# Three products of zeros ahead of the first loads, one load issued by ScalarE, and all scaled copies of the mixing on VectorE

## The chip, the cores and the metric

The kernel runs on one core of one Trainium2 chip. The core has four engines that compute, each with a queue of its own that it works off in order: TensorE (PE in the profile, its weight loads PEld), VectorE (DVE), ScalarE (ACT) and GpSimd (POOL). SyncE (SP) issues the transfers between HBM and the core's own memory (SBUF); PE writes its results to PSUM, in eight banks. Engines wait for each other by semaphores. The metric is the time of one execution on the device, in microseconds, the median of several runs.

## The reference

An attention without softmax is followed by a channel mix.

```python
def _attn_ref(q, k, v):
    scores = scale * np.matmul(q, k.transpose(0, 1, 3, 2)) - np.log(S)
    attn = 1.0 / (1.0 + np.exp(-scores))
    return np.matmul(attn, v)
...
def _moe_ref(x, mu_k, mu_r, w_k, w_v, w_r):
    x_prev = np.concatenate([np.zeros((B, 1, D)), x[:, :-1, :]], axis=1)
    xk = mu_k * x + (1.0 - mu_k) * x_prev
    xr = mu_r * x + (1.0 - mu_r) * x_prev
    k = np.maximum(xk @ w_k, 0.0)
    v = k * k @ w_v
    r = 1.0 / (1.0 + np.exp(-(xr @ w_r)))
    return r * v
```

The shapes: 8 batches, 12 heads, 448 positions, 64 elements a head, so 768 channels; `w_k` is 768 x 1024, `w_v` 1024 x 768, `w_r` 768 x 768, and the weights come as 64-bit floats.

## The kernel before

The 96 heads are laid out as 48 pairs of heads (n), two heads of 64 elements on the 128 partitions, with positions along the free axis. The kernel has two phases, each with a plan of its own.

**Attention.** The loop (lines 460 to 475) takes two pairs, n and n + 1, at a time and seven steps j over the 448 keys, 64 at a time. `score` (line 309) issues four matmuls, whose quarters fill the 128 x 128 array together, into one of two PSUM buffers `sc`, and ACT makes the sigmoid of both halves into one of three buffers `pf` (line 320). `weigh` (line 325), two steps behind, multiplies `pf` with the values `vn` and sums over the seven steps in a PSUM bank `av`; there are four such banks, so a bank is written again two rounds later. Operands here are fp32, and each call of matmul leaves two records on PE and two weight loads.

After the last step of a round `gather` (line 336) mixes each pair with its predecessor in time, once with `mu_r` and once with `mu_k`: POOL clears the first column of a buffer `xo` (a ring of eight), a scaled copy of `av`, shifted by one column, is written to it (line 345 on DVE for `mu_r`, line 347 on ACT for `mu_k`), DVE adds `mu * av` (line 348), and a transfer stores the result to HBM. Beside this, DVE turns the 64-bit weights into fp32 bits (lines 212 to 216) and forms sums of their quarters (line 244). For the first weight, `w_r`, ACT casts the rounded part into a `slot` (line 289) and DVE makes the rest (line 290). Spare time is given to the first operands of the second phase (lines 413 and 414).

**Products.** Three products with `w_r`, `w_k` and `w_v` (stages 0 to 2), each over four slices s of two batches, run as seven half-sized products each (`multiply`, line 518), every one as three passes of rounded and remaining parts. Their sums are taken from PSUM by DVE and ACT (`evacuate`, line 558).

**What sets the order.** Nothing is issued as the loops run. Each operation is given to a `Plan` with its engine, its cost in ns, its priority (lower first), and the buffers that it reads and writes. `order` (line 49) plays the plan through: an engine that is free takes the ready operation of the lowest priority number; a result is ready for another operation `WAIT` = 170 ns after its producer's planned end (none from PE to PE), and a transfer after a modelled 300 GB/s and 1300 ns. The operations are then issued in the order of their planned starts, which sets each engine's queue. Semaphores are put in by the framework from what each operation reads and writes, so the plan decides order alone.

**The start.** The framework's own preamble ends near 0.7 us. Then DVE clears a small tile `warm` (line 141) and ACT makes a sigmoid of it (line 142), which has its table loaded early. All transfers are issued by SP through `dma` (line 200), 500 ns each in the plan. `load` (line 297) brings one pair: the first 64 key columns with all queries (512 columns, 256 KB), the remaining keys (384 columns, 192 KB), and the values (224 KB). For the first two pairs `late` orders them: both first pieces, both second pieces, both values. The first score step needs the first pieces of pairs 0 and 1, the next one the second pieces too.

Of the kernel before, what the change touches and what calls it, by code (L numbers as in the profile page):

```python
# [10 lines left out]
AF = mybir.ActivationFunctionType  # L11
# [11 lines left out]
class Plan:  # L23
# [7 lines left out]
    def op(self, engine, cost, prio, run, reads, writes, dma=None):  # L31
        i = len(self.ops)
        deps = set()
        for r in reads:
            if r in self.writer:
                deps.add(self.writer[r])
        for w in writes:
            if w in self.writer:
                deps.add(self.writer[w])
            deps.update(self.readers.get(w, ()))  # L40
        for r in reads:
            self.readers.setdefault(r, []).append(i)
        for w in writes:
            self.writer[w] = i
            self.readers[w] = []
        deps.discard(i)
        self.ops.append(Op(engine, cost, prio, run, deps, dma))

    def order(self):
        import heapq  # L50
        ops = self.ops
        left = [len(o.deps) for o in ops]
        users = [[] for _ in ops]
        for i, o in enumerate(ops):
            for d in o.deps:
                users[d].append(i)
        at = [0.0] * len(ops)
        free, ready, waiting = {}, {}, []
        for i, o in enumerate(ops):
            free[o.engine] = 0.0  # L60
            ready.setdefault(o.engine, [])
            if not left[i]:
                heapq.heappush(waiting, (0.0, i))
        bus, start = self.bus, {}
        now = 0.0
        while len(start) < len(ops):
            while waiting and waiting[0][0] <= now:
                i = heapq.heappop(waiting)[1]
                heapq.heappush(ready[ops[i].engine], (ops[i].prio, i))
            for e in free:  # L70
                if free[e] <= now and ready[e]:
                    i = heapq.heappop(ready[e])[1]
                    o = ops[i]
                    start[i] = now
                    free[e] = now + o.cost
                    end = now + o.cost
                    if o.dma is not None:
                        bus = max(bus, end + 700) + o.dma
                        end = bus + 1300
                    for u in users[i]:  # L80
                        gap = 0 if ops[u].engine == e == "PE" else self.WAIT
                        at[u] = max(at[u], end + gap)
                        left[u] -= 1
                        if not left[u]:
                            heapq.heappush(waiting, (at[u], u))
            nxt = [free[e] for e in free if ready[e]] + ([waiting[0][0]] if waiting else [])
            if nxt:
                now = max(now, min(nxt)) if min(nxt) > now else now
        self.start = start
        return sorted(start, key=lambda i: (start[i], i))  # L90
# [8 lines left out]
def attention_then_channel_mix(  # L99
# [15 lines left out]
    nc = tc.nc  # L115
    P = 128
# [3 lines left out]
    D = v.shape[-1]  # L120
# [17 lines left out]
    dram = ctx.enter_context(tc.tile_pool(name="dram", bufs=1, space=DRAM))  # L138

    warm = const.tile([P, 2], F32, name="warm")  # L140
    nc.vector.memset(warm, 0.0)
    nc.scalar.activation(warm[:, 1:], warm[:, :1], AF.Sigmoid)
    mur = const.tile([P, NJ], F32, name="mur")
    muk = const.tile([P, NJ], F32, name="muk")
    omr = const.tile([P, NJ], F32, name="omr")
# [2 lines left out]
    xr_d = [dram.tile([P, NJ, S], F32, name=f"xr_d{b}") for b in range(B)]  # L148
# [8 lines left out]
    def ring(pool, name, bufs, shape, dtype):  # L157
        return [pool.tile(shape, dtype, name=f"{name}{i}") for i in range(bufs)]
# [14 lines left out]
    av = ring(psum, "av", 4, [P, 512], F32)  # L173
    sc = ring(psum, "sc", 2, [P, 2, 512], F32)

    raw = ring(apool, "raw", RAW, [P, 2 * S], F32)
    vn = ring(apool, "vn", RAW, [P, NV, D], F32)
    pf = ring(apool, "pf", PFB, [P, 2, S], F32)
    xo = ring(apool, "xo", 8, [P, S], F32)

    plan = Plan()
    op = plan.op
    SP, PE, ACT, DVE, POOL = "SP", "PE", "ACT", "DVE", "POOL"
# [4 lines left out]
    def act(n, sbuf=False, ptr=False):  # L188
        return 51 + 0.834 * n + 42 * sbuf + 93 * ptr

    def dve(n, fast=False, ptr=False):
        return 69 + n / (1.92 if fast else 0.96) + 61 * ptr
# [7 lines left out]
    def dma(dst, src, prio, reads, writes):  # L200
        ns = dst.shape[0] * math.prod(dst.shape[1:]) * 4 / 300
        op(SP, 500, prio, lambda: nc.sync.dma_start(dst, src), reads, writes, dma=ns)
# [94 lines left out]
    def load(n, at):  # L297
        i = n % RAW
        late = 0.5 * (n < 2)
        for a, c in enumerate((slice(0, D + S), slice(D + S, 2 * S))):  # L300
            dma(raw[i][:, c], qk[n][:, c], at + late * a, [], [("raw", i, a)])
        dma(vn[i], v[n], at + 2 * late, [], [("vn", i)])

    half = [slice(h * D, (h + 1) * D) for h in range(2)]
# [17 lines left out]
    def bank(m):  # L322
        return m % 4
# [12 lines left out]
    def gather(n, at):  # L336
        b, j = divmod(n, NP)
        x, X = av[bank(n)], ("av", bank(n))
        for mu, om, dst, key in ((mur, omr, xr_d, "xr_d"), (muk, omk, xk_d, "xk_d")):
            u = nxo[0] % len(xo)  # L340
            nxo[0] += 1
            y, Y = xo[u], ("xo", u)
            op(POOL, 200, at, lambda y=y: nc.gpsimd.memset(y[:, 0:1], 0.0), [], [Y])
            if key == "xr_d":
                op(DVE, dve(S, ptr=True), at, lambda y=y, om=om: nc.vector.tensor_scalar_mul(y[:, 1:], x[:, :S - 1], om[:, j:j + 1]), [X, ("om", key)], [Y])  # L345
            else:
                op(ACT, act(S, ptr=True), at, lambda y=y, om=om: nc.scalar.mul(y[:, 1:], x[:, :S - 1], om[:, j:j + 1]), [X, ("om", key)], [Y])  # L347
            op(DVE, dve(S, ptr=True), at, lambda y=y, mu=mu: nc.vector.scalar_tensor_tensor(y, x[:, :S], mu[:, j:j + 1], y, ALU.mult, ALU.add), [X, Y], [Y])  # L348
            dma(dst[b][:, j], y, at, [Y], [(key, n)])

# [93 lines left out]
    for n in range(4):  # L444
        load(n, -9 + n // 2 * 2)
# [14 lines left out]
    for t in range(T + LAG):  # L460
        n, j = t // NV * 2, t % NV
        if t < T:
            if j == 0:
                for _ in range(1 + (n % 6 == 4)):
                    convert_next(n + 4, n - 2 if n else None)
            score(n, j, t, n + j / NV)
        if t < LAG:
            continue
        n, j = (t - LAG) // NV * 2, (t - LAG) % NV
        weigh(n, j, t - LAG, n + j / NV)  # L470
        if j == NV - 1:
            for m in (n, n + 1):
                gather(m, m)
                if m + 4 < N:
                    load(m + 4, n + 0.5)
# [22 lines left out]
    op = plan.op  # L498
# [89 lines left out]
    at = 0  # L588
# [49 lines left out]
```

## Time and profile before

| What | Value |
|---|---|
| Time, median of 3 runs | 824.85 us (824.68 to 825.09) |
| Time of the profiled execution | 824.86 us |
| Its span, first to last instruction | 823.1 us |
| Instructions | 15181 |
| Read from HBM, written to it | 109.06 MB, 69.73 MB |

The span is what the profile shows; some 1.8 us of the execution's time lie outside it. In the profile a group is a line of the kernel with its engine, operation and tiles; behind "idle before" stands what ended the idle time of the engine ahead of it. A timeline's row gives the start and the length in us, the engine, the line and the tiles, and how many instructions were merged into it. A row of a window table gives the window, its length, and per engine the busy time with the number of records that lie in it, wholly or in part. A matmul's record is longer than the distance to the next one, since matmuls overlap.

### The profile page before, as it was taken

The page shows a single profiled execution, that of the slowest core. Times are in us where ns is not written, and L with a number is a line of the kernel's source. Part 1 is how long each engine was busy: PE and PEld are TensorE (multiplying, and loading weights), DVE is VectorE, ACT ScalarE, POOL GpSimd, SP SyncE. Part 2 cuts the span into 40 slices and gives each one's busy share as a digit, 9 for nine tenths or more (in the row PEclk, how much of TensorE's full clock was granted, in tenths as well). Part 3 has the DMA queues.
Part 4 walks back from the last instruction along what each step waited for, and adds up shares of the span by engine and source line. Part 5 has one row for each costly group of instructions (what it writes and reads, how often), then busy time and mean ns, then how long its engine had stood idle before and what let it go on. Part 6 is the DMA issues. An engine that isn't in the chain of part 4 may idle for free.

```text
span 823.1 us, 15181 instructions
## 1 busy us (share of the span) xinstructions
PE 812.9 (99%) x5460; PEld 622.9 (76%) x5460; DVE 615.1 (75%) x1152; ACT 467.1 (57%) x791; POOL 10.3 (1%) x100
## 2 busy tenths in 40 slices
PE   8999999999999999999999999999999999999997
PEld 3433334343334999999999999999999999999997
DVE  0888687685654898989999639376697795977955
ACT  5788776767676553546584747647694233333320
POOL 0000000000000000000000000000000000000000
PEclk9999999999999999999999999999999999999999
DMA  8787789999872948576879542422865545755414
GB/s 274 267 312 265 268 272 317 335 352 308 287 262 90 304 161 264 169 247 206 328 228 316 195 146 102 151 96 102 288 217 188 164 145 190 225 179 178 143 39 156
DMA packets 94715, 179.80 MB, mean 218 GB/s; under 512 B 10544, under 2 KB 75312, under 8 KB 94640
## 3 DMA queue, kind: packets, MB, share of 16 engines
q1 hardware_dynamic: 94640, 178.83, 64.7%
q8 instruction: 43, 0.70, 0.4%
q14 instruction: 32, 0.26, 0.1%
HBM read 109.06 MB, written 69.73 MB: 217 GB/s over the span
## 4 chain that ended last, share of the span: by engine, by line
PE 90%; DVE 4%; ACT 2%; DMA 2%; issue 1%; SPq 0%; ACTq 0%; DVEq 0%
PE xb L530 39%; PE yb L530 29%; PE sc L317 12%; PE av L329 11%; DVE xo L348 1%; ACT pf L320 1%; DMA raw<-in_qk 1%; ACT xo L347 1%; DMA wraw<-in_moe_w_r 1%; DVE wbit L216 0%; DVE wbit L215 0%; DVE wbit L214 0%; DVE xo L345 0%; DMA wk_o<-wbit 0%; DVE wbit L244 0%
## 5 line engine op out<-in xcount | busy, mean ns | idle before, releaser
L530 PE MATMUL xb<-rra,slot 128*128 128x448 f32 x1188 | 249.8, 362 | 0.0
L530 PEld LDWEIGHTS xb<-rra,slot 128*128 128x128 f32 x1188 | 222.7, 188 | 15.5 <-issue 0.7
L530 PE MATMUL yb<-rra,slot 128*128 128x448 f32 x927 | 193.0, 362 | 0.0
L320 ACT ACTIVATE pf<-sc 128x896 f32<-128x896 f32 x168 | 152.1, 918 | 58.9 <-PE sc L317 58.8
L530 PEld LDWEIGHTS yb<-rra,slot 128*128 128x128 f32 x927 | 173.8, 187 | 11.6
L317 PE MATMUL sc<-raw 64*64 64x448 f32 x1344 | 165.6, 545 | 5.4 <-DMA raw<-in_qk 3.5
L329 PE MATMUL av<-pf,vn 64*64 64x448 f32 x1344 | 162.3, 537 | 0.0
L317 PEld LDWEIGHTS sc<-raw 64*64 64x64 f32 x1344 | 52.0, 134 | 84.9 <-issue 57.0
L329 PEld LDWEIGHTS av<-pf,vn 64*64 64x64 f32 x1344 | 54.0, 133 | 74.9 <-issue 73.6
L530 PE MATMUL xb<-rrb,slot 128*128 128x448 f32 x396 | 89.1, 362 | 0.0
L345 DVE TENSOR_SCALAR xo<-av,omr 128x447 f32<-128x447 f32 x48 | 32.5, 681 | 73.6 <-PE av L329 47.1
L413 ACT CAST rra<-ysa 128x448 fp32r<-128x448 f32 x104 | 56.6, 562 | 50.5 <-PE yb L530 21.9
L530 PEld LDWEIGHTS xb<-rrb,slot 128*128 128x128 f32 x396 | 74.2, 187 | 5.0
L414 DVE TENSOR_TENSOR rra<-ysa,rra 128x448 fp32r<-128x448 f32 x102 | 59.6, 617 | 10.4 <-ACT rra L413 10.3
L530 PE MATMUL yb<-rrb,slot 128*128 128x448 f32 x261 | 57.5, 362 | 0.0
L530 PEld LDWEIGHTS yb<-rrb,slot 128*128 128x128 f32 x261 | 48.9, 187 | 3.3
L413 ACT CAST rra<-ysb 128x448 fp32r<-128x448 f32 x58 | 31.4, 564 | 34.2 <-PE yb L530 19.2
L568 DVE TENSOR_TENSOR u<-yb,p1s 128x448 f32<-128x448 f32 x40 | 24.9, 622 | 30.5 <-PE yb L530 30.1
L566 ACT COPY p1s<-xb 128x448 f32<-128x448 f32 x40 | 21.2, 530 | 39.9 <-PE xb L530 39.5
L413 ACT CAST rra<-wbit 128x448 fp32r<-128x448 f32 x46 | 24.4, 566 | 29.7 <-PE yb L530 29.1
L414 DVE TENSOR_TENSOR rra<-ysb,rra 128x448 fp32r<-128x448 f32 x54 | 31.4, 617 | 13.0 <-ACT rra L413 13.0
L548 ACT ACTIVATE cc<-cc 128x448 f32<-128x448 f32 x48 | 27.5, 577 | 19.8 <-DVE cc L574 13.5
(59 smaller groups left out, 712.9 us busy)
## 6 DMA issues: line engine op xcount, KB each, us to landing
k_d<-cc SPq DMA_DIRECT2D x64, 224.0 KB, 2.1
raw<-in_qk SPq DMA_DIRECT2D x48, 256.0 KB, 4.1
vn<-in_v SPq DMA_DIRECT2D x48, 224.0 KB, 5.3
xr_d<-xo SPq DMA_DIRECT2D x48, 224.0 KB, 3.5
xk_d<-xo SPq DMA_DIRECT2D x48, 224.0 KB, 3.4
r_d<-cc SPq DMA_DIRECT2D x48, 224.0 KB, 2.0
out<-cc SPq DMA_DIRECT2D x48, 224.0 KB, 3.1
raw<-in_qk SPq DMA_DIRECT2D x48, 192.0 KB, 4.5
```

Of the source, the lines that this page charges most:

```text
L317: nc.tensor.matmul(u[half[h ^ (m % 2)], m % 2, :S], x[half[h], c], x[half[h], D:D + S], start=True, stop=True)
L320: op(ACT, act(2 * S), at, lambda: nc.scalar.activation(f, u[:, :, :S], AF.Sigmoid, bias=NEG_LOG_S, scale=SCALE), [("sc", t % 2)], [("pf", ...
L329: nc.tensor.matmul(av[bank(m)][half[r ^ (m % 2)], :S], vn[m % RAW][half[r], j, :], pf[t % PFB][half[r], m % 2, :], start=j == 0, stop=j == ...
L345: op(DVE, dve(S, ptr=True), at, lambda y=y, om=om: nc.vector.tensor_scalar_mul(y[:, 1:], x[:, :S - 1], om[:, j:j + 1]), [X, ("om", key)], [Y])
L347: op(ACT, act(S, ptr=True), at, lambda y=y, om=om: nc.scalar.mul(y[:, 1:], x[:, :S - 1], om[:, j:j + 1]), [X, ("om", key)], [Y])
L348: op(DVE, dve(S, ptr=True), at, lambda y=y, mu=mu: nc.vector.scalar_tensor_tensor(y, x[:, :S], mu[:, j:j + 1], y, ALU.mult, ALU.add), [X, ...
L413: op(ACT, act(TB, True), at, lambda t=t: nc.scalar.copy(hi[t], y[:, t]), [Y[t]], [H[t]])
L414: op(DVE, dve(TB), at, lambda t=t: nc.vector.tensor_sub(lo[t], y[:, t], hi[t]), [Y[t], H[t]], [L[t]])
L530: nc.tensor.matmul(bank, a, b, start=first and t == 0 and e == 0, stop=t == n - 1 and e == 2, skip_group_check=True)
L548: op(ACT, act(TB), at, lambda: nc.scalar.activation(c, src, AF.Relu), R, [C])
L566: op(ACT, act(TB), at, lambda: nc.scalar.copy(p1s[i], x), [X], [P1])
L568: op(DVE, dve(TB), at, lambda: add(u2[i], y, p1s[i]), [Y, P1], [U2])
```

## The change

There are four edits.

1. In the planner, what PE produces is ready for other engines 370 ns after its planned end, in place of 170.
2. Behind the allocation of the tiles and ahead of the plan, DVE clears 256 columns of `xo[0]`, and PE multiplies them with themselves three times (128 x 128 weights, 256 columns, fp32) into the bank `av[3]`, which nothing reads before it is written anew. The clearing of `warm` and its sigmoid move behind this.
3. The first piece of pair 1 (256 KB) is issued by ACT, ahead of its sigmoid of `warm`, and no longer by SP; it is no longer in the plan.
4. The shifted scaled copies for `mu_k` (448 columns, one for each of the 48 pairs) go from ACT to DVE, as those for `mu_r` stand already.

```diff
-                        gap = 0 if ops[u].engine == e == "PE" else self.WAIT
+                        gap = 0 if ops[u].engine == e == "PE" else self.WAIT + 200 * (e == "PE")
...
     warm = const.tile([P, 2], F32, name="warm")
-    nc.vector.memset(warm, 0.0)
-    nc.scalar.activation(warm[:, 1:], warm[:, :1], AF.Sigmoid)
...
+    nc.scalar.dma_start(raw[1][:, :D + S], qk[1][:, :D + S])
+    zero = xo[0][:, :256]
+    nc.vector.memset(zero, 0.0)
+    for _ in range(3):
+        nc.tensor.matmul(av[3][:, :256], zero[:, :P], zero, start=True, stop=True)
+    nc.vector.memset(warm, 0.0)
+    nc.scalar.activation(warm[:, 1:], warm[:, :1], AF.Sigmoid)
...
         for a, c in enumerate((slice(0, D + S), slice(D + S, 2 * S))):
-            dma(raw[i][:, c], qk[n][:, c], at + late * a, [], [("raw", i, a)])
+            if (n, a) != (1, 0):
+                dma(raw[i][:, c], qk[n][:, c], at + late * a, [], [("raw", i, a)])
...
-            if key == "xr_d":
-                op(DVE, dve(S, ptr=True), at, lambda y=y, om=om: nc.vector.tensor_scalar_mul(y[:, 1:], x[:, :S - 1], om[:, j:j + 1]), [X, ("om", key)], [Y])
-            else:
-                op(ACT, act(S, ptr=True), at, lambda y=y, om=om: nc.scalar.mul(y[:, 1:], x[:, :S - 1], om[:, j:j + 1]), [X, ("om", key)], [Y])
+            op(DVE, dve(S, ptr=True), at, lambda y=y, om=om: nc.vector.tensor_scalar_mul(y[:, 1:], x[:, :S - 1], om[:, j:j + 1]), [X, ("om", key)], [Y])
```

## The prediction

> **What bounds the kernel now.** I read the page first: who is busy, and which chain ends last.
>
> ```profile
> PE 812.9 (99%) x5460; PEld 622.9 (76%) x5460; DVE 615.1 (75%) x1152; ACT 467.1 (57%) x791; POOL 10.3 (1%) x100
> PE 90%; DVE 4%; ACT 2%; DMA 2%; issue 1%; SPq 0%; ACTq 0%; DVEq 0%
> ```
>
> PE bounds everything, so a gain can come only from time in which PE waits or runs slowly. A window table splits the span where attention ends and the products begin, and where the last matmul ends (columns: length, busy time and records of PE, PEld, DVE, ACT, POOL, granted clock, DMA share, GB/s).
>
> ```profile
> 0.00:263.66 263.66, 258.22 (x2689) 103.18 (x2689) 174.38 (x322) 188.77 (x246) 10.27 (x100) 1.00 0.82 282
> 263.66:818.34 554.68, 554.68 (x2776) 519.68 (x2772) 439.49 (x828) 278.34 (x545) 0.00 (x0) 1.00 0.58 190
> 111.41:200.10 88.69, 88.69 (x948) 35.65 (x944) 62.79 (x109) 61.59 (x76) 4.14 (x36) 1.00 0.92 318
> ```
>
> In the products PE is busy for all of 554.68 us: 2772 matmuls, 0.200 us each, no hole. Nothing can be gained there, only lost. In attention a step (one score or one weigh, four calls of matmul) leaves 8 records. The third row is a stretch without a hole: its 88.69 us hold 118 steps (948/8, less the pieces at the edges), so a step takes 0.752 us. Attention has 336 steps (the first row's 2689 records are theirs and one of the products), 252.5 us at that rate. It lasts from the first matmul at 3.51 (below) to 263.66, 260.15 us. So **7.6 us** is the most that this change can reach, beside an earlier start. The timeline shows where its first part lies.
>
> ```profile
> 0.72 1.28 ACT L142 ACT_TABLE_LOAD   x1 [0.72 <-PEq L614]
> 0.72 0.33 POOL L343 MEMSET xo<- 128x1 f32 x8 [0.29 <-POOLq L614]
> 0.73 1.81 SPq L202 DMA_DIRECT2D raw<-in_qk  x4
> 0.80 0.06 DVE L141 MEMSET warm<- 128x2 f32 x1 [0.80 <-PEq L614]
> 3.51 0.29 PEld L317 LDWEIGHTS sc<-raw 64*64 64x64 f32 x4 [3.51 <-DMA raw<-in_qk]
> 4.16 0.29 PEld L317 LDWEIGHTS sc<-raw 64*64 64x64 f32 x4 [0.36 <-DMA raw<-in_qk]
> 5.96 0.92 ACT L320 ACTIVATE pf<-sc 128x896 f32<-128x896 f32 x1 [3.74 <-PE sc L317]
> 6.25 0.29 PEld L317 LDWEIGHTS sc<-raw 64*64 64x64 f32 x4 [0.76 <-DMA raw<-in_qk]
> ...
> 6.93 1.82 PE L317 MATMUL sc<-raw 64*64 64x448 f32 x8
> 8.48 0.89 PE L329 MATMUL av<-pf,vn 64*64 64x448 f32 x2
> 9.20 0.57 PE L329 MATMUL av<-pf,vn 64*64 64x448 f32 x4
> 9.58 0.54 PE L317 MATMUL sc<-raw 64*64 64x448 f32 x2
> ```
>
> The third step takes 8.48 - 6.93 = 1.55 us, twice a later one; records fall from 0.89 to 0.57 us between 8.48 and 9.20. PE runs at half speed until about 9.1 (the granted clock of the windows shows none of it: 1.00). Four steps are done by 9.58, 6.07 us after the start, where 3.01 would do: **3.06 us** of excess.
>
> The rest, 7.6 - 3.1 = 4.5 us, are holes later on. I cut windows of PE at the step starts around each.
>
> ```profile
> 28.40:30.13 1.73, 1.73 (x22) 1.00 0.79 237
> 31.63:33.71 2.08, 1.87 (x20) 1.00 0.84 309
> 38.22:40.03 1.81, 1.74 (x21) 1.00 0.94 270
> 41.53:45.47 3.94, 3.32 (x37) 1.00 1.00 381
> 65.01:67.27 2.26, 1.74 (x21) 1.00 0.91 334
> 92.82:94.72 1.90, 1.73 (x20) 1.00 0.90 266
> 103.74:105.54 1.80, 1.74 (x20) 1.00 0.91 276
> 107.05:110.48 3.43, 3.31 (x37) 1.00 0.93 320
> 214.20:216.10 1.90, 1.74 (x21) 1.00 0.93 279
> ```
>
> Each holds two steps (four where x37). Length less steps gives 0.23, 0.58, 0.31, 0.93, 0.76, 0.40, 0.30, 0.42, 0.40: 4.33 us. What stood ahead of the late sigmoid on ACT (first the casts' group with its idle time, then the timeline):
>
> ```profile
> L289 ACT CAST slot<-wbit 128x384 fp32r<-128x384 f32 x21 | 10.7, 511 | 5.9 <-DVE wbit L216 5.4
> ...
> 30.89 1.16 ACT L347 ACTIVATE xo<-av,omk 128x447 f32<-128x447 f32 x2 [0.40 <-DVE xo L345]
> ...
> 37.84 0.51 ACT L289 CAST slot<-wbit 128x384 fp32r<-128x384 f32 x1 [1.40 <-DVE wbit L216]
> ...
> 42.58 1.22 ACT L347 ACTIVATE xo<-av,omk 128x447 f32<-128x447 f32 x2 [0.33 <-DVE xo L345]
> ...
> 64.45 1.16 ACT L347 ACTIVATE xo<-av,omk 128x447 f32<-128x447 f32 x2 [0.54 <-DVE xo L345]
> ...
> 213.28 1.16 ACT L347 ACTIVATE xo<-av,omk 128x447 f32<-128x447 f32 x2 [0.86 <-DVE xo L345]
> ```
>
> In four windows (31.63, 41.53, 65.01, 214.20) two scaled copies stand ahead of it, by the rows, and I take the one at 107.05 so too: 0.58 + 0.93 + 0.76 + 0.42 + 0.40 = **3.09 us**. In the other four I put a weight cast there, by the row at 37.84 for the second: 0.23 + 0.31 + 0.40 + 0.30 = 1.24 us.
>
> **The change part by part.** *The copies go to DVE.* ACT loses 48 copies, one a pair of heads, and with them what it waited for in its queue: the holes of 3.09 us. What is late next on ACT is the cast (below). On DVE 48 operations are added, behind which the conversions queue. The two engines also waited for each other over these copies:
>
> ```profile
> DVE xo L345 <- ACT xo L347: 24.0, 20, 1.9
> ...
> 18.81 0.68 DVE L345 TENSOR_SCALAR xo<-av,omr 128x447 f32<-128x447 f32 x1 [7.14 <-PE av L329]
> 20.72 0.68 DVE L345 TENSOR_SCALAR xo<-av,omr 128x447 f32<-128x447 f32 x1 [1.22 <-ACT xo L347]
> 21.32 0.68 DVE L348 SCALAR_TENSOR_TENSOR xo<-av,mur,xo 128x448 f32<-128x448 f32 x1
> 23.68 0.36 DVE L212 TENSOR_SCALAR wbit<-wraw 128x384 uint32<-128x384 uint32 x1
> ```
>
> The mixing of two pairs of heads holds DVE from 18.81 to 23.68, 4.87 us, of which 1.22 us is waiting for ACT. Eight operations in a row at 0.60 us (20.72 to 21.32) take 4.8 us. Where that hand-over stands (20 waits, 24.0 us in all), DVE pays nothing for the added work; 48 x 0.60 = 28.8 us are added and 24.0 given back. So I cost DVE at +4.8 us spread over an attention in which it is busy 174.38 of 263.66 us: nothing on PE's path. Without that cover the added work is paid in late casts, the slow rival below.
>
> *Late casts.* They wait for a DVE that idled at hand-overs. Bounds: all of their 1.24 us goes, or casts take the copies' place (the second rival). I take -0.4, nearer to the 1.24 us of now, since the casts stay in ACT's queue.
>
> *Zeros.* The memset of 256 columns starts at about 0.80 in place of the one there; between 0.06 us (2 columns) and 0.36 (384), I take 0.3. PE starts at 1.2, and after a first weight load (0.29 for 64 columns) multiplies from 1.5. A cold step is two rounds of records, 1.55/2 = 0.78 us for 448 columns, so 256 columns take 0.44; three calls are six records: 2.7 us. Estimate: zeros end at 4.2; bounds 2.9 (at full speed) and 6.0 (if each record also waits for its weights, 0.29 each). The first true step waits for that: 4.3 in place of 3.51, though its second half started at 4.16 anyway. When does PE speed up? Before, 5.6 us after its first matmul, or 4.5 without the 0.36 and 0.76 us in which it waited for loads; from 1.5 that is 6.0 to 7.1. Then: step 0 runs from 4.3 to 5.85; its sigmoid starts 1.8 us after the second half of the step, as before (4.16 to 5.96), and with 0.92 ends at 7.0; step 1 needs the last piece of the first loads, at 6.25 before and some 0.45 earlier now, and ends at 6.7 (7.3 in the late case); step 2 waits for the sigmoid and runs from 7.0 (7.3) to 7.8 (8.1); the first weigh ends at 8.55 (8.8). Before it was 9.58: **-1.0 us**. Bounds: -1.8 (the second sigmoid, 0.92 after step 1, gates step 3 at 7.8) and +0.3 (cold until 9.1 all the same).
>
> *The load on ACT.* SP issues one transfer every 0.45 us (1.81/4); all later ones move up by that, already counted. ACT pays one such issue ahead of its table load (1.28), which then ends near 2.5; the sigmoid at 5.96 covers it, else 0.45. POOL's eight memsets now queue behind the zeros, whose tile they clear; only the mixing at 18.81 needs them.
>
> [...]
>
> *The planner's 200 ns* change orders alone. In the products PE has no hole; the tightest spot that I found:
>
> ```profile
> 402.86 0.62 DVE L574 TENSOR_TENSOR cc<-xb,cc 128x448 f32<-128x448 f32 x1
> ...
> 404.18 5.56 PE L530 MATMUL xb<-rra,slot 128*128 128x448 f32 x27
> ```
>
> DVE ends at 403.48, 0.70 us before PE writes that bank. One more operation ahead (0.62) still fits, a second makes a hole of 0.5. I take 0; the upper end is 12 such spots (three rows in four slices), 6 us; below nothing it can't go, as there is no hole.
>
> **Sum:** the profiled execution took 824.86 us (span 823.08, 1.78 around it), 0.01 over the median. 824.86 - 1.0 - 3.1 - 0.4 = **820.4 us**.
>
> **The rivals.** *The warm-up pays nothing* (zeros don't raise the speed, or delay step 0 as much as they give). For it: PE needed 5.6 us before; against: in 2 of these it was waiting. It gives 820.4 + 1.0 to 1.3, about 821.5.
>
> [...]
>
> *The holes only move.* The sigmoid then waits behind casts, since ACT, freed, gets more of them in one place and DVE more work ahead of them: the casts' 1.24 us triples. For it: four holes stand behind casts already. Against: the hand-overs that make DVE late go. 824.86 - 1.0 - 3.1 + 2.5 = 823.3, no change.
>
> *DVE becomes the bound* (slower).
>
> ```profile
> 30.00:50.00 20.00, 19.10 (x202) 7.59 (x198) 18.46 (x38) 16.21 (x25) 0.99 (x8) 1.00 0.83 288
> ```
>
> Here DVE is already busy 18.46 of 20 us; two mixings fall into these 20 us (one each 14 steps, 10.5 us), and their four added operations (0.68) make 21.2. If the backlog doesn't drain, each of the 21 casts of the first weight is late by more than the 1.40 us that cost 0.31 at 38.22: 21 x 0.4 = 8.4 us in place of 1.24, so 824.86 - 4.1 + 7.2 = 828.0. It decides from a cast wait of about 1.4 us on. Against: after 200 DVE is far from full.
>
> *The products get holes*: 820.4 + up to 6, about 824 at half of it.
>
> **How the numbers follow.** Forecast 0.58, no gain from the warm-up 0.17, holes that only move 0.12, DVE the bound 0.07, holes in the products 0.06. A measurement of this kernel tells about 0.2% (1.65 us) from no change, so faster is below 823.2. Faster: 0.58 + 0.17 and a little of the third, 0.77; same 0.13; slower 0.10. Range: from 819.0 (all casts' holes gone, or the front at its bound) to 823.4, which takes in the second and third case; the last two are left out.
>
> **What would show it.** Right: a step of 0.75 us before 7.1, the fourth step done by 8.9; no hole behind an L347; DVE's mixing still 4.8 us; the products at 554.7 us. Wrong: steps of 1.55 us until 9; ACT idle for DVE ahead of L289 by far more than 5.4 us; idle PE in the products.

## The result, and the profile after

| | Before | Changed |
|---|---|---|
| Median of 6 runs each | 824.80 us (824.45 to 825.09) | 820.57 us (819.44 to 820.70) |
| Ratio, 95% interval | | 0.9946 (0.9933 to 0.9959) |
| Profiled execution, span | 824.86, 823.1 us | 820.33, 818.5 us |

The forecast was 820.4 us. The window table of the changed kernel, cut at the same events as before (first matmul of the products, end of the last one):

```profile
0.00:258.47 258.47, 256.70 (x2695) 105.08 (x2695) 198.62 (x368) 166.98 (x200) 10.30 (x100) 1.00 0.84 287
258.47:813.68 555.21, 555.20 (x2776) 519.50 (x2772) 440.84 (x831) 277.51 (x543) 0.00 (x0) 1.00 0.58 189
813.68:818.54 4.86, 0.00 (x0) 0.00 (x0) 1.25 (x2) 0.00 (x0) 0.00 (x0) 0.98 0.21 77
```

Attention ends 5.19 us earlier (263.66 to 258.47). The products take 0.53 us more (554.68 to 555.21), the end 0.12 us more (4.86 against 823.08 - 818.34 = 4.74). -5.19 + 0.53 + 0.12 = -4.54 us is the whole difference of the spans.

Where the 5.19 us of attention come from is read in two views. First PE's timeline of the start (score is line 324 now, weigh 336, the zeros 183):

```profile
1.18 2.93 PE L183 MATMUL av<-xo 128*128 128x256 f32 x6 [1.18 <-DVE warm L184]
4.43 2.56 PE L324 MATMUL sc<-raw 64*64 64x448 f32 x16 [0.32 <-DMA raw<-in_qk]
7.25 0.98 PE L324 MATMUL sc<-raw 64*64 64x448 f32 x8 [0.27 <-ACT pf L327]
8.05 0.93 PE L336 MATMUL av<-pf,vn 64*64 64x448 f32 x8
```

The zeros run from 1.18 to 4.11. The first true step follows at 4.43, and what it waits for is its load, not the zeros. The first two steps take 2.56 us with their tail, the third and fourth about 0.8 us each. So PE is at full speed by the third step; by the lengths of the records (1005 ns at 4.43, 537 ns at 5.97) it is so from 6.0 on. The fourth step is done at 8.81, 0.80 us earlier than before (9.61 by the same count, the start of the 33rd record). The other 4.39 us are the holes later on: summed over all steps between the fourth and the last, what a step took over 0.752 us was 4.41 us before and is 0.02 us now. The waits show why:

```profile
ACT pf L327 <- PE sc L324: 88.7, 150, 3.6
ACT L185 <- PEq L618: 1.2, 1, 1.2
```

These are all waits of ACT up to 259 us. It waits for scores, as it should, and no longer for DVE, neither ahead of a copy nor ahead of a cast. DVE's mixing of two pairs of heads, which had taken 4.87 us with 1.22 us of waiting, runs without a gap:

```profile
18.04 0.68 DVE L351 TENSOR_SCALAR xo<-av,omr 128x447 f32<-128x447 f32 x1 [6.50 <-PE av L336]
...
22.19 0.68 DVE L352 SCALAR_TENSOR_TENSOR xo<-av,muk,xo 128x448 f32<-128x448 f32 x1
22.78 0.35 DVE L218 TENSOR_SCALAR wbit<-wraw 128x384 uint32<-128x384 uint32 x1
```

Eight operations from 18.04 to 22.78 are 4.74 us, with two copies more than before in less time.

### The profile page after: what moved, and what is told of

It is laid out like the page before. It is cut to its first block, busy times and chain, and to the rows that moved or that the text cites. A ratio compares the mean times of both kernels' runs of the same rounds, so it can differ in the third digit from the quotient of the medians.

```text
span 818.5 us, 15184 instructions
## 1 busy us (share of the span) xinstructions
PE 811.9 (99%) x5466; PEld 624.6 (76%) x5466; DVE 640.7 (78%) x1201; ACT 444.5 (54%) x743; POOL 10.3 (1%) x100
## 4 chain that ended last, share of the span: by engine, by line
PE 99%; DMA 0%; DVE 0%; ACT 0%; issue 0%
PE xb L534 39%; PE yb L534 29%; PE sc L324 15%; PE av L336 15%; DMA raw<-in_qk 0%; ACT pf L327 0%; DVE cc L586 0%; DVE cc L559 0%
## 5 line engine op out<-in xcount | busy, mean ns | idle before, releaser
L327 ACT ACTIVATE pf<-sc 128x896 f32<-128x896 f32 x168 | 154.0, 917 | 89.0 <-PE sc L324 88.7
L324 PE MATMUL sc<-raw 64*64 64x448 f32 x1344 | 157.3, 539 | 0.6 <-DMA raw<-in_qk 0.3
L336 PE MATMUL av<-pf,vn 64*64 64x448 f32 x1344 | 156.2, 536 | 0.0
L336 PEld LDWEIGHTS av<-pf,vn 64*64 64x64 f32 x1344 | 51.4, 133 | 74.9 <-issue 74.4
```

The lines of the kernel that those rows point to most:

```text
L324: nc.tensor.matmul(u[half[h ^ (m % 2)], m % 2, :S], x[half[h], c], x[half[h], D:D + S], start=True, stop=True)
L327: op(ACT, act(2 * S), at, lambda: nc.scalar.activation(f, u[:, :, :S], AF.Sigmoid, bias=NEG_LOG_S, scale=SCALE), [("sc", t % 2)], [("pf", ...
L336: nc.tensor.matmul(av[bank(m)][half[r ^ (m % 2)], :S], vn[m % RAW][half[r], j, :], pf[t % PFB][half[r], m % 2, :], start=j == 0, stop=j == ...
```

## The experiments

Twelve kernels were run. Theory A was that of the prediction: copies in ACT's queue, and the two engines' waiting for each other over them, make the holes, and the zeros pay about 1 us at the start. In the table "full speed" is worked out from the lengths of the records around the change of speed, "fourth step" is the time when it is done, "holes" the sum over the later steps of attention as above, all from one profile each. Times are compared with the kernel before of the same row, since its own median moves between 824.10 and 824.87 us from one comparison to the next. The time is the median of 4 to 10 runs, beside that of the kernel before in the same comparison.

| Kernel | Time (before) | Ratio, 95% interval | Full speed | Fourth step | Holes | Products |
|---|---|---|---|---|---|---|
| before | | | 9.2 | 9.61 | 4.41 | 554.68 |
| changed | 820.57 (824.80) | 0.9946 (0.9933 to 0.9959) | 6.0 | 8.81 | 0.02 | 555.21 |
| copies_only | 820.21 (824.49) | 0.9948 (0.9933 to 0.9962) | 8.8 | 9.47 | 0.02 | 554.68 |
| front_only | 824.13 (824.49) | 0.9996 (0.9986 to 1.0005) | 5.5 | 8.54 | 4.45 | 554.68 |
| wait_only | 824.03 (824.49) | 0.9989 (0.9980 to 0.9998) | 7.7 | 8.91 | 4.25 | 554.67 |
| no_wait | 820.19 (824.49) | 0.9947 (0.9933 to 0.9962) | 5.3 | 8.34 | 0.79 | 554.67 |
| wait_attention | 819.90 (824.10) | 0.9945 (0.9930 to 0.9960) | 4.8 | 8.20 | 0.19 | 554.67 |
| no_zeros | 820.13 (824.10) | 0.9949 (0.9934 to 0.9964) | 8.2 | 9.30 | 0.15 | 554.68 |
| no_actload | 819.60 (824.10) | 0.9946 (0.9929 to 0.9962) | 5.6 | 8.41 | 0.02 | 554.69 |
| all_on_act | 833.07 (824.10) | 1.0104 (1.0089 to 1.0119) | 7.8 | 9.05 | 13.53 | 554.68 |
| split_by_pair | 820.88 (824.87) | 0.9949 (0.9935 to 0.9962) | 7.9 | 9.06 | 1.00 | 554.68 |
| after_again | 820.15 (824.87) | 0.9941 (0.9926 to 0.9956) | 7.2 | 9.10 | 0.21 | 554.68 |
| one_zero | 820.47 (824.87) | 0.9945 (0.9932 to 0.9959) | 8.1 | 9.27 | 0.02 | 554.68 |
| best_of_parts | 819.91 (824.87) | 0.9939 (0.9927 to 0.9952) | 4.7 | 8.19 | 0.72 | 554.68 |

### The four edits one by one

**copies_only**: the kernel before with the fourth edit alone.

```diff
-            if key == "xr_d":
+            if key:
```

> The scaled copies go to DVE, the other three edits are left out. Theory A (copies in ACT's queue make the holes of PE, and the two engines' waiting for each other makes DVE late for the casts): 4.4 us of holes between 9.6 and 264 shrink to under 1.0, the fourth step is done at 9.6 as before, the products take 554.7, so 820.4 to 821.7 us. Rival B (the 200 ns of the planner take the holes away by another order): at least 3 us of holes stay, 823.5 to 825.

The 4.41 us of holes are gone to 0.02, the front and the products are as before, and the time falls by 4.28 us, to 0.2 us below what was expected. The rest of the change isn't needed for any of that. The whole change gained 4.23 us in its comparison, so by the times this edit is the whole gain, and what the other three add was not shown. The casts' holes went with those behind the copies: ACT waited 5.4 us for DVE ahead of casts before, and now, by its waits up to 259 us, 0.3:

```profile
ACT pf L320 <- PE sc L317: 89.5, 151, 4.0
ACT L142 <- PEq L614: 0.7, 1, 0.7
ACT slot L289 <- DVE wbit L244: 0.3, 1, 0.3
```

**front_only**: the kernel before with edits 2 and 3, the zeros and the load on ACT, and nothing else.

> Zeros and the load on ACT alone; the copies stay on ACT and the planner keeps 170 ns. Theory A: the fourth step is done at 8.8 in place of 9.6, the holes later on stay within 0.5 of 4.4 us, products 554.7, so 823.5 to 824.5 us. Rival C (an earlier start is used up by a later wait for loads or for DVE): attention ends within 0.3 us of 263.66 and the time stays at 824.8.

The fourth step is done at 8.54, the holes stay at 4.45, and attention ends at 262.63, 1.03 us earlier. So nothing later in attention uses that up. Over ten runs the ratio is 0.9996 (0.9986 to 1.0005), so the timing does not tell the gain from none; the start without zeros scatters too, as the next run shows.

**wait_only**: the kernel before with edit 1.

> The planner's 200 ns alone. Theory A: the holes behind the copies stay (3 us or more), and the products get the new hole of 0.5 us, so 824.5 to 825.8 us. Rival B: the holes shrink to under 1.5 us, so 821.5 to 822.5 us.

The holes stay (4.25 in all, two of them with other sizes), so the 200 ns don't take them away. The expected hole of 0.5 us in the products isn't there, and the time is 0.5 us below the range that was expected. The fourth step is done at 8.91 in place of 9.61 although nothing in the start was edited: PE came to speed at 7.7, by itself.

**no_wait**: the changed kernel without edit 1.

```diff
-                        gap = 0 if ops[u].engine == e == "PE" else self.WAIT + 200 * (e == "PE")
+                        gap = 0 if ops[u].engine == e == "PE" else self.WAIT
```

> The changed kernel with 170 ns in the planner again. Theory A: no hole behind a copy, at most 0.5 us behind casts, products without a hole at 554.7, so 819.8 to 820.8 us. Rival B: holes of 2 us or more return in attention, so 822 us or more. If the hole of 0.5 us in the products doesn't go, it isn't the planner's.

There are two holes, 0.79 us in all. ACT's timeline ahead of the second:

```profile
56.77 1.03 ACT L420 CAST rra<-ysa 128x448 fp32r<-128x448 f32 x2 [1.08 <-DMA ysa<-xr_d]
57.71 0.91 ACT L327 ACTIVATE pf<-sc 128x896 f32<-128x896 f32 x1
58.51 0.50 ACT L295 CAST slot<-wbit 128x384 fp32r<-128x384 f32 x1
58.92 0.92 ACT L327 ACTIVATE pf<-sc 128x896 f32<-128x896 f32 x1
```

Casts of operands for the second phase, which the planner puts into ACT's spare time, wait 1.08 us for a load, and the sigmoid waits behind them. What ACT waits for here is neither a copy nor a weight cast, and the 0.79 us are more than the 0.5 that was expected. The 200 ns are not what keeps such holes away: copies_only has 170 ns and none, best_of_parts has 200 ns in attention and 0.72 us behind casts of both kinds. The changed kernel itself, with one order, had 0.02 us in its first profile and 0.21 in its second, where ACT waited 0.59 us for such a load. So these holes come and go with the order and with the landing of loads, 0.0 to 0.8 us.

### The place in the queue, or the wait

That the copies make the holes could mean two things: two copies more stand ahead of a sigmoid, or ACT stands still ahead of them, waiting for DVE. Two kernels tell them apart.

**all_on_act**: the kernel before with all copies on ACT.

```diff
-            if key == "xr_d":
+            if False:
```

> The kernel before with both scaled copies of each mixing on ACT, none on DVE (170 ns, no zeros, all loads on SP). Theory A (what is ahead of the sigmoid in ACT's queue makes the holes): four copies of 0.63 us stand ahead of it a round in place of two, and holes behind copies grow to 6 us or more, 827 us or more. Rival E (the hand-over between ACT and DVE is what costs, not the place of the copies): only one hand-over a round is left as before, the holes stay at 4 to 5 us, 824.5 to 825.5.

**split_by_pair**: the kernel before with the copies dealt out by pairs, 48 on each engine as before.

```diff
-            if key == "xr_d":
+            if n % 2 == 0:
```

> The kernel before with the copies dealt out otherwise: both copies of an even pair on DVE, both of an odd pair on ACT (48 each, as before), so that neither engine's copies read a bank whose copies the other one makes. If the place in ACT's queue makes the holes: two copies a round still stand ahead of a sigmoid, 3 us or more of holes, 823.4 us or more. If what ACT waits for DVE ahead of its copies makes them: ACT's idle time ahead of L347 falls from 7.3 to under 2 us and the holes from 4.4 to under 2 us, 820.5 to 822.5 us.

In all_on_act a round looks like this on ACT and on PE:

```profile
97.28 0.63 ACT L347 ACTIVATE xo<-av,omr 128x447 f32<-128x447 f32 x1
97.80 0.64 ACT L347 ACTIVATE xo<-av,omk 128x447 f32<-128x447 f32 x1
98.31 0.65 ACT L347 ACTIVATE xo<-av,omr 128x447 f32<-128x447 f32 x1
98.83 0.65 ACT L347 ACTIVATE xo<-av,omk 128x447 f32<-128x447 f32 x1
99.34 1.75 ACT L320 ACTIVATE pf<-sc 128x896 f32<-128x896 f32 x2
```

```profile
99.17 0.93 PE L329 MATMUL av<-pf,vn 64*64 64x448 f32 x8
100.34 0.98 PE L317 MATMUL sc<-raw 64*64 64x448 f32 x8 [0.25 <-ACT pf L320]
```

Four copies start 0.52 us apart and hold ACT for 2.06 us (97.28 to 99.34), without a wait. PE's step at 100.34 starts 1.17 us after the one before, 0.42 late, and 19 of the 24 rounds have a hole of this size. The holes grew to 13.53 us and the time to 833.07, as theory A expected and more; rival E expected no growth and falls. So the place in ACT's queue alone makes holes when enough stands in it: some 1.6 us (2.06 - 0.42) can stand ahead of a sigmoid without one, as long as ACT isn't late already. Two copies, 1.04 us, fit. With 0.3 to 0.9 us of waiting ahead of them, as before the change, they come to 1.4 to 1.9 us, at the edge or over it.

Of the five holes that the prediction put down to copies, only the last, with a wait of 0.86 us, comes about in this way alone. In the rounds of the other four, ACT had casts ahead of the previous sigmoid as well (in its timeline at 29.17, 40.28, 62.06 and 105.79), and in the fourth of them no wait stands ahead of the copies at all. ACT had run without a pause since a cast that waited for DVE:

```profile
103.36 0.51 ACT L289 CAST slot<-wbit 128x384 fp32r<-128x384 f32 x1 [1.40 <-DVE wbit L216]
...
107.67 1.15 ACT L347 ACTIVATE xo<-av,omk 128x447 f32<-128x447 f32 x2
```

So a round has a hole when copies, casts and what ACT waits for DVE ahead of either come to too much together.

split_by_pair tells what the waits are worth in this. Its ACT still makes 48 copies, two of them in a row each round, and these are its groups up to 264 us:

```profile
L347 ACT ACTIVATE xo<-av,omk 128x447 f32<-128x447 f32 x24 | 15.3, 637 | 0.0
L347 ACT ACTIVATE xo<-av,omr 128x447 f32<-128x447 f32 x24 | 15.1, 628 | 1.3 <-PE av L329 1.3
```

No idle time for DVE stands ahead of a copy. In the kernel before, ACT's waits had this row:

```profile
ACT xo L347 <- DVE xo L345: 7.3, 15, 0.9
```

The holes fall from 4.41 to 1.00 us, and the time by 3.99 us to 820.88. In DVE's waits of this kernel there is none for L347 any more, and ACT waits for DVE ahead of a cast once, 1.4 us in all, where it was 5.4 us before. Both engines still read the four `av` banks, but no longer with copies from the same one. What is left of the holes follows on that one wait, directly and behind the next two copies, with ACT never idle in between:

```profile
36.74 0.51 ACT L289 CAST slot<-wbit 128x384 fp32r<-128x384 f32 x1 [1.41 <-DVE wbit L216]
```

So with two copies a round on ACT, what cost was the two engines' waiting for each other over one bank, and the casts that came late by it. That the copies may stand anywhere is not shown: four of them a round on ACT cost 9.0 us with no wait ahead of them.

L345 and L347 only read `av`, in all 128 partitions, and write different buffers, and yet in the kernel before they waited for each other, 24.0 and 7.3 us. Why two readers of one bank wait for each other is not shown, and no run here tried them unguarded.

### The start

**no_zeros**: the changed kernel without the zeros; **one_zero**: with one product in place of three; **no_actload**: with the first piece of pair 1 on SP again.

```diff
-    zero = xo[0][:, :256]
-    nc.vector.memset(zero, 0.0)
-    for _ in range(3):
-        nc.tensor.matmul(av[3][:, :256], zero[:, :P], zero, start=True, stop=True)
```

> The changed kernel without the three products of zeros and their memset; the load stays on ACT. If the zeros bring PE to speed: the first step starts near 4.4 and PE speeds up 4.1 to 5.6 us later, at 8.5 to 10.0, so the fourth step is done near 10 in place of 8.8 and the time is 1.0 to 1.6 us above the changed kernel, 821.4 to 822.2. If they do nothing (rival): the fourth step is done at 8.8 and the time is within 0.3 us of the changed kernel.

> The changed kernel with one product of zeros in place of three: PE is busy from 1.2 to 2.0 and then idle until the loads land at 4.4. If work without a break is what brings PE to speed: it speeds up as without zeros, at 8.0 or later, fourth step done at 9.3. If any work in the first microseconds does it: at 4.8 to 5.8 as with three, fourth step at 8.2 to 8.8.

```diff
-            if (n, a) != (1, 0):
-                dma(raw[i][:, c], qk[n][:, c], at + late * a, [], [("raw", i, a)])
+            dma(raw[i][:, c], qk[n][:, c], at + late * a, [], [("raw", i, a)])
...
-    nc.scalar.dma_start(raw[1][:, :D + S], qk[1][:, :D + S])
```

> The changed kernel with the first piece of pair 1 on SP again. If the two loads issued together delay each other: the first piece lands at 3.5 in place of 4.4, the first step starts at 4.15, right behind the zeros, but the second pieces land at 6.1 in place of 5.5 and take the gain back: fourth step done at 8.3 to 8.8, time within 0.5 us of the changed kernel. If the load on ACT is what helps the front: fourth step at 9.2 or later, 0.5 us or more above it.

PE's timeline of one_zero (columns as before):

```profile
1.18 1.22 PE L183 MATMUL av<-xo 128*128 128x256 f32 x2 [1.18 <-DVE warm L184]
4.44 4.33 PE L324 MATMUL sc<-raw 64*64 64x448 f32 x24 [2.04 <-DMA raw<-in_qk]
8.52 1.01 PE L336 MATMUL av<-pf,vn 64*64 64x448 f32 x8
```

One product of zeros, followed by 2.04 us of idling, does nothing in its one profile: the three score steps take from 4.44 to 8.52, and full speed comes at 8.1, as without any zeros (8.2). Three products, which fill the time to 4.11, bring it at 4.7 to 7.2 in the seven profiles that have them. By these profiles zeros count as work when three products of them fill the time. Whether one product falls short by the break behind it or by being less work was not told apart. That zeros help is not shown by the times. The kernel before of the same comparison was 3.97 us above no_zeros and 4.40 above one_zero, and 4.23 and 4.72 above the changed kernel, where 1.0 us or more was expected between no_zeros and the changed kernel. In the profile no_zeros is done with its fourth step at 9.30, where near 10 was expected; that is 0.49 us later than the changed kernel. It has none of its 0.53 us of holes in the products.

With the load on SP, the first piece lands earlier and the first step starts at 4.04, right behind the zeros, in place of 4.43. Its fourth step is done at 8.41, as expected, and its time is 4.50 us below the kernel before, where the changed kernel's was 4.23: no loss, so the load on ACT is not what helps the front. The two first pieces issued together landed later than in line behind each other: with both issued at 0.73, they landed at 4.4 and 4.6 in the changed kernel's profile, in line at 3.5 and 4.2 in this one, near those of the kernel before (3.47 and 4.11). The second pieces then land by 6.3 in place of 5.5 (6.20 before). Why the later of the two first pieces, too, lands later than in line isn't shown.

### The products, and a version from the parts

**wait_attention** has the 200 ns in the attention's plan alone; **after_again** is the changed kernel, unedited; **best_of_parts** is wait_attention with the load on SP again.

```diff
-                        gap = 0 if ops[u].engine == e == "PE" else self.WAIT + 200 * (e == "PE")
+                        gap = 0 if ops[u].engine == e == "PE" else self.WAIT + self.late * (e == "PE")
...
-    plan = Plan()
+    plan = Plan(late=200)
...
-    plan = Plan()
+    plan = Plan(late=0)
```

> The changed kernel, but the planner's 200 ns in the attention's plan alone, 170 ns throughout in that of the products. Theory A: attention without a hole as in the changed kernel (ends near 258.5 of the profile's span), and the products without the 0.53 us of holes at 361 to 364, so 0.5 us below the changed kernel: 819.7 to 820.3 us. Rival D (that hole comes from a late transfer alone, whatever the order): it stays, 820.2 to 820.8.

> The changed kernel once more, unedited. If the 0.53 us of holes in the products belong to its order and its early start: they are there again, at 361 to 364. If they came with one execution's transfers: products at 554.7 us, without a hole. PE's change of speed again between 4.8 and 5.8.

> Zeros, both copies on DVE, all loads on SP, and the 200 ns in the attention's plan alone. Theory A: no hole in attention or in the products, fourth step done at 8.2 to 8.5, so 819.4 to 820.0 us, 0.5 to 1 us below the changed kernel. Rival: the parts don't add up (the order changes with each), 820.3 or more.

The 0.53 us of holes in the products stand in the first profile of the changed kernel alone, around 361 to 364 us. The second one has 554.68 us there, as every other kernel has within 0.01 us:

```profile
258.95:813.63 554.68, 554.68 (x2776) 519.61 (x2772) 440.47 (x831) 277.26 (x543) 0.00 (x0) 1.00 0.58 190
```

In the first, by the waits, DVE had stood still for 4.0 us until a store of a converted weight landed, and was then late with the sums that empty the banks:

```profile
DVE wbit L218 <- DMA wv_o<-wbit: 4.0, 1, 4.0
```

Its timeline there:

```profile
360.58 0.62 DVE L578 TENSOR_TENSOR cc<-xb,cc 128x448 f32<-128x448 f32 x1
```

That sum ends at 361.20, 0.15 us before the next product writes its bank at 361.35, 0.17 us late; this is the kind of spot at which 0.70 us were left before. The unedited kernel run again waited 2.8 us in place of 4.0 for this store and has no hole, so it came with one execution's transfers and not with the order alone. Rival D had the cause, a late transfer, but the hole didn't stay. wait_attention, without the hole, is at 819.90 us, and best_of_parts at 819.91, 0.24 below the changed kernel of its comparison, where 0.5 to 1 us was expected. best_of_parts has 0.72 us of holes in attention in place of none. No version was shown to be faster than the changed kernel.

## Why the prediction was right

The time was forecast at 820.4 us and measured at 820.57. The mechanism of the main term was right; that the number came so close is in part luck, since in the profile the holes gave 0.9 us more than forecast, and the front, the products and the end together 0.85 us less.

- **What bounds.** Right: PE's 7.6 us of excess in attention was all that could be gained, and the profile shows 5.19 us of it.
- **The copies, -3.1 us.** Right, and shown by copies_only. What the step gave as the cause, the copies in ACT's queue and what ACT waited for in it, was narrowed: split_by_pair keeps 48 copies there and loses three quarters of the holes, so the wait decided. One of the five holes, 0.42 us at 107.05, was put there by assumption; its copies had no wait, and ACT was late from a cast.
- **The casts, -0.4 us.** Mis-sized: their 1.24 us went wholly. I took them nearer to no change because they stay in ACT's queue. But they had waited for a DVE that was late from its own waits for ACT, and split_by_pair bears this out: with the same work on DVE and without these waits, ACT waits 1.4 us ahead of casts in place of 5.4. The rival by which holes only move fell: ACT's waits for DVE are 0.
- **DVE.** Right: 4.74 us for the mixing, where 4.8 was forecast, so the 48 added operations cost nothing on PE's path. The slow rival rested on a backlog at 30 to 50 us, and the same view of waits excludes it.
- **The front, -1.0 us.** The mechanism was right, the size too large: -0.80 us in the profile, and less over all profiles. The fourth step is done at 8.20 to 9.10 in the five with three zeros and the load on ACT (median 8.54), and at 8.91 to 9.61 in the five with neither (median 9.06), so 0.5 us is nearer. No timing shows any of it: the ratio of front_only holds 1 in its interval. The zeros' end was forecast at 4.2 (4.11), full speed at 6.0 to 7.1 (6.0 here, 4.7 to 7.2 in all).
- **The load on ACT.** The forecast moved every landing up by 0.45 us. That holds roughly for the second pieces, 0.1 and 0.7 us earlier than before, and fails for the first: these land 0.9 and 0.5 us later. The zeros fill the time until 4.11 and the first step starts at 4.43, so this cost little.
- **The scatter of the change of speed.** It falls at no fixed distance from the first work: 3.5 to 6.0 us after the first matmul in the seven profiles with three zeros, 3.8 to 5.7 in the six without any. The rival without a gain from the warm-up is then no other case but the late end of the same one; after_again, which is the changed kernel once more, at 7.2 (4.8 to 5.8 was expected), comes near it with a fourth step at 9.10. What sets the moment was not shown.
- **The planner, 0.** Right for the time: wait_only keeps 4.25 of 4.41 us of holes. In attention the order and the landing of loads decide over 0 to 0.8 us of holes behind casts.
- **Products, 0.** 0.53 us in the profile and 0 in the next one.

So the sum reads: -0.80 (forecast -1.0), -4.39 (-3.5), +0.53 (0), +0.12 at the end (0). The last 0.12 us lie behind the issue of the last store, 3.52 us from the end in place of 3.39. All seven profiles with three zeros have 4.86 to 4.88 us behind the last matmul, the others 4.73 to 4.74; why is open, but it takes back a part of what the zeros give.

## What to carry to other kernels

Look at what an engine waits for ahead of a group, not only at the group's busy time: two short operations a round did little harm in ACT's queue where they did not wait for another engine's reading of the same bank (1.00 us of holes in split_by_pair, against 4.41 us with 7.3 us of such waits before the change), and dealing out the copies so that one engine makes all those of a bank was worth nearly as much (3.99 us) as taking them off ACT (4.28 us). Where a holder-up is removed, count the second row of waiters in full: here DVE, which no longer waited for ACT's copies, caught up as well, and ACT's waits for DVE ahead of casts fell from 5.4 to 0.3 us in copies_only. A gain of half a microsecond at a start whose change of speed itself falls anywhere within 2.5 us (4.7 to 7.2) could be read in these profiles, but not in timings, not even in the ten of front_only (0.9986 to 1.0005).

## What the runs showed of the hardware

Zeros count as work for PE's change of speed: with three products from 1.18 to 4.11 it came at 4.7 to 7.2 us, 3.5 to 6.0 us after the first of them (seven profiles), and with data alone 3.8 to 5.7 us after the first matmul (six). One product, to 2.40, did not bring it before 8.1 (one profile). The granted clock doesn't show the change: it is 1.00 from 0 to 5 and from 5 to 10 us in the kernel before and in the changed one. The lengths of the score records do (951 to 1007 ns in the first two steps of the kernel before, 536 from 9.58 on). Two loads of 256 KB issued at the same moment by two engines landed at 4.4 and 4.6 us, where one ahead of the other gave 3.47 and 4.11 in the kernel before: 0.9 and 0.5 us later, in one profile each.
